# The first gating of a gated recurrence and feed-forward kernel: 384 tokens in halves of 192 instead of 512 in halves of 256

## The chip, the cores and the metric

The kernel runs on one core of one Trainium2 chip. The metric is device time in microseconds (us) of a whole execution: before the change 511.12 us, the median of three runs (511.03 to 511.22). The five engines have short names in the profile: PE is TensorE, DVE is VectorE, ACT is ScalarE, POOL is GpSimd, and SP is the engine whose queue issues nearly all the transfers here. PEld is TensorE's loading of weights.

## The reference

A gated linear recurrence runs over 4 sequences of 5824 tokens with 256 channels, and its output goes through a feed-forward network in which two projections are multiplied.

```python
log_a = 8.0 * sigmoid(r_gate) * log(clip(sigmoid(a_param)))
a_t = exp(log_a)
x_gated = sqrt(max(1 - a_t * a_t, 1e-6)) * sigmoid(i_gate) * x
h = a_t[:, t] * h + x_gated[:, t]      # for every token t; h is 0 at a sequence's start
h_ffn = (h @ w1) * (h @ w2) @ w3       # 256 -> 1024, 1024 -> 1024
out = h_ffn @ w_out                    # 1024 -> 256
```

## The kernel before, in words

All 23296 tokens stand in one row and are cut into chunks. Chunks 0 and 1 have 256 tokens each, chunks 2 to 45 have 512, and chunk 46 has 256. Chunks 0 and 1 are gated together: they share their loads, their gates and their buffers (`gates_of`, `width`), but root, gating product, scan and cast are done for each half by itself, so that the first half can go on to TensorE while the second is scanned.

Matrices w3 and w_out are multiplied with each other once, on the chip ("folding"), so that a chunk needs two stages of matmuls: up, with w1 and w2, and down, with the folded product. Channels lie on partitions and tokens run along the free axis; a gate is loaded with tokens on partitions and is turned, either by TensorE (chunks in `TURN_R` and `TURN_U`) or by a transposing transfer.

Nothing in the order is automatic. The string `ORDER` lists every job, and each engine and the transfer queue take their jobs in that order. A job's letter, its chunk and its part make a word:

- `r`, `i`, `x` load the three inputs (L151), `Lw1.1` and the like load half of w1 or w2, half of w_out, or an eighth of w3 into a staging buffer (L407). All of these are issued by SP, one after another.
- `Cw..` casts a staged weight to bf16: on ACT (L414) if in `W_ACT`, on DVE (L416) if in `W_DVE`, else on POOL.
- `R`, `I` are the two tanh, `V`, `U` the turns (L200 on TensorE), `d` the exponential (L223), `s` the square (L231, L233), `q` the root (L238), `p`, `t` build i_gate's part times x (L173, L192), `g` is the gating product (L248, L251), `h` the scan (L270), `y` the cast of the scan (L280, L282).
- `a`, `b` are the up matmuls with w1 and w2 (L299) of a quarter of the 1024 columns, `c` moves a's sums out of PSUM (L320, L322), `m` multiplies them with b's (L337), `D` is the down stage (L357), `e` and `o` move its sums out and store them.
- `Ft`, `Fc`, `Fm`, `Fe` fold one eighth of w3: transpose (L425), copy, product with w_out (L436), and scaling into `wp_sb` (L470, L472). Every `D` needs all eight.
- `W` is two matmuls on the identity (L287), whose results nobody reads.

Sets such as `DV_COPY`, `AC_SQUARE` or `DV_CAST` say which engine takes a job. `HALVED` says for how many of the four quarters the up stage of chunks 0 and 1 is run half by half; the other quarters wait for both halves and take the whole width. `RINGS` gives the number of buffers: the PSUM ring `po` has four, shared by `a`, turns, folding and `D`, and `pb` has two, shared by `b` and `W`; a job that takes a slot waits until the slot's last reader is done.

Of the kernel before, what the change touches and what calls it, by code (L numbers as in the profile page):

```python
# [23 lines left out]
def kernel(  # L24
# [25 lines left out]
    CT = 512  # L50
    sizes = [256, 256] + [512] * 44 + [256]
# [44 lines left out]
    FOLD_ACT = {('e', 0), ('e', 4), ('e', 5), ('e', 7)}
    FOLD_DMA = set()
    W_ACT = {('w2', 0), ('w3', 3)}
    W_DVE = {('w1', 1)}
# [4 lines left out]
    HALVED = 4  # L104
# [24 lines left out]
    def width(c):  # L129
        return CT if c == 0 else sizes[c]  # L130

    def part(c):
        return slice(sizes[0], CT) if c == 1 else slice(0, sizes[c])
# [37 lines left out]
    def plus(c):  # L171
        t = T["thi", c][:, :sizes[c] // P, :]
        (nc.vector if c in DV_PLUS else nc.gpsimd).tensor_scalar(t, t, 1.0, 1.0, op0=ALU.add, op1=ALU.mult)  # L173

# [115 lines left out]
    def in_half(c, mp):  # L290
        return c < 2 and mp < HALVED

# [181 lines left out]
    def last(c):  # L474
# [21 lines left out]
        r0 i0 x0 Lw1.1 Lw1.0 r2 i2 Lw2.0 Lw3.2 x2 E W13 A3. A0. A1. A2. R0.1 R0.0 W3 W10 V0.0 V0.1 I0 t0.1 d0.0 s0.0  # L496
        d0.1 s0.1 q0.0 t0.0 Cw1.1 q0.1 Cw1.0 R2 I2 W5 W8 W0 U0 W4 W11 W6 W12 W7 W9 W2 g0 h0.1 h0.0 y0.1 y0.0 a0.0.1
        a0.1.1 a0.1.0 a0.0.0 V2 W15 Cw2.0 g1 h1.1 h1.0 y1.1 y1.0 d2.1 Lw2.1 Lwo.1 Lwo.0 r3 Cw3.2 d2.0 s2.1 s2.0 q2
        b0.0 c0.0.0 c0.1.0 a1.1.0 m0.0 Ft2 a1.1.1 c1.1.0 b0.1 a1.0.0 a0.2.1 a1.0.1 b1.1 m0.1 Fc2 b1.0 a0.2.0 p2 t2.0
        t2.1 U2 c1.0.0 m1.1 Cw2.1 m1.0 a0.3.1 W14 b0.2 a1.3.1 W1 a1.3.0 c0.2.0 g2 Cwo.1 Cwo.0 r4 Lw3.0 Lw3.5 i3 Lw3.1  # L500
        Lw3.4 x3 Lw3.3 Lw3.6 Lw3.7 r7 m0.2 h2.0 h2.1 R3 a1.2.1 a1.2.0 a0.3.0 c1.3.0 c0.3.0 Fm2 b0.3 b1.2 V3 R4 V4
        c1.2.0 d3.1 d4.0 d3.0 d4.1 m0.3 b1.3 y2 Fe2 m1.2 m1.3 a2.0.0 a2.0.1 b2.0 a2.1.0 c2.0.1 c2.0.0 c2.1.0 m2.0
        Cw3.0 s3.1 Cw3.5 Cw3.1 b2.1 a2.2.1 Ft0 a2.1.1 Fc0 Ft1 c2.1.1 Fc1 s4.0 I3 s4.1 c2.2.1 a2.2.0 Ft5 Fm0 p3 Cw3.4
        c2.2.0 Fc5 m2.1 s3.0 q3 Cw3.3 Fe0 b2.3 Fm1 q4 Fe1 Ft4 t3.0 t3.1 U3 Fc4 g3 h3.0 h3.1 Cw3.6 Cw3.7 b2.2 Fm5 Fm4
        a2.3.1 Ft7 R7 Fe5 Fe4 Fc7 r5 i4 r6 x4 i5 i6 i7 c2.3.1 a2.3.0 Ft3 R5 I4 c2.3.0 Fc3 Ft6 Fm7 y3 a3.2.1 Fc6 Fm3
        m2.3 R6 Fe7 c3.2.1 V7 m2.2 Fe3 d7.1 a3.2.0 c3.2.0 d7.0 b3.2 Fm6 a3.3.1 a3.0.0 a3.3.0 m3.2 Fe6 c3.0.0 I5 c3.3.1
        s7.0 I6 V5 r8 i8 V6 r9 x5 b3.3 d5.1 a3.0.1 d5.0 c3.0.1 c3.3.0 m3.3 p4 t4.0 t4.1 p5 s7.1 U4 a3.1.1 c3.1.1 s5.0
        I7 I8 D0.1 D0.0 b3.0 b3.1 a3.1.0 g4 h4.0 h4.1 s5.1 R8 R9 d6.0 d6.1 p6 y4 p8 t5.0 t5.1 D0.3 D0.2 m3.0 e0.0
        c3.1.0 a4.1.1 b4.1 a4.3.1 D2.0 D2.1 s6.1 q7 e2.0 q5 s6.0 x6 p7 t6.0 t6.1 c4.1.1 e0.1 m3.1 c4.3.1 x7 x8 o0.0
        i10 r11 V9 o2.0 a4.0.1 a4.1.0 c4.0.1 c4.1.0 m4.1 a4.2.0 b4.3 a4.3.0 U5 g5 h5.0 h5.1 c4.2.0 c4.3.0 q6 D2.3 D2.2  # L510
        e2.1 r12 r10 V8 o2.1 o0.1 i9 i11 x10 a4.0.0 U6 D3.0 a4.2.1 D3.1 b4.0 c4.0.0 I10 c4.2.1 e3.0 d9.1 d9.0 m4.3 g6
        y5 t8.1 t7.1 t7.0 m4.0 a5.1.0 b4.2 a5.1.1 a5.0.1 a5.0.0 b5.0 c5.1.1 c5.1.0 c5.0.0 m4.2 h6.1 U7 a5.3.1 c5.0.1
        s9.1 R10 c5.3.1 R11 d8.1 I9 m5.0 g7 h6.0 b5.1 D3.3 b5.3 D3.2 a5.2.1 a5.3.0 e3.1 R12 d8.0 m5.1 c5.2.1 c5.3.0
        h7.1 D4.2 a5.2.0 D4.3 e4.1 m5.3 i13 V10 o3.0 x9 p10 t8.0 y6 p9 s8.0 s9.0 h7.0 b6.0 a6.0.0 a6.0.1 y7 c5.2.0 I11
        I13 a6.2.1 a6.2.0 b5.2 s8.1 c6.0.0 c6.0.1 c6.2.0 D4.1 a6.1.0 D4.0 d10.1 c6.2.1 d10.0 e4.0 q9 a6.1.1 m6.0 m5.2
        U8 o3.1 i12 r15 V11 r13 t9.1 t9.0 U9 V12 a6.3.0 b6.1 c6.1.1 c6.1.0 m6.1 a6.3.1 b6.2 a7.1.1 b6.3 a7.1.0 m6.2
        t10.0 s10.1 p11 t10.1 o4.0 o4.1 r16 i14 i16 c6.3.0 q8 c6.3.1 m6.3 g8 h8.0 h8.1 g9 c7.1.1 c7.1.0 a7.3.0 a7.0.0
        a7.0.1 b7.1 c7.3.0 R15 c7.0.0 c7.0.1 D6.0 D6.1 a7.3.1 D5.0 D6.2 b7.3 D6.3 D5.1 d11.1 c7.3.1 e6.0 s11.1 I12
        d11.0 d12.1 m7.1 h9.1 y8 a7.2.1 a8.2.0 b7.0 e6.1 m7.3 p12 s11.0 p13 s10.0 e5.0 a8.2.1 a7.2.0 c7.2.1 I16 c8.2.1
# [145 lines left out]
```

## Time and profile before

| | us |
|---|---|
| median of three runs | 511.12 |
| the profiled execution itself | 510.87 |
| its span (first to last instruction) | 509.1 |
| TensorE busy, of which | 501.7 |
| matmuls on the identity (`W`) | 10.7 |
| ACT busy | 461.5 |
| DVE busy | 431.8 |
| POOL busy | 318.0 |

The profiled execution took 1.8 us more than its span, and stands 0.25 us under the median. TensorE's busy time includes the `W` matmuls, so 99% busy does not mean 99% useful. A matmul's printed duration overlaps with the next one's: matmuls in a row start closer together than they last. The same holds to a smaller degree for the other engines: copies of 512 columns on DVE print 0.68 us and start 0.60 us apart. Sums of work are therefore made from the distance between starts.

### The profile page before, as it was taken

The numbers are of one execution on the slowest core, as the hardware profiler recorded it, in microseconds if no ns is written. First come the engines' busy times: TensorE is split into PE (matmuls) and PEld (weight loads), VectorE is DVE, ScalarE is ACT, GpSimd is POOL, SyncE is SP. The second block draws the span as 40 slices with busy tenths as digits, with TensorE's granted clock in tenths as the row PEclk, the third lists the DMA queues.
The fourth block names the chain that finished last, engine by engine and source line by source line (L and its number), as shares of the span: only waits on it lengthen the run. The fifth ranks groups of instructions, "written<-read, shape, count | busy, mean of one in ns | idle before, by whom it ended". The sixth has DMA issues, their size and how long they took to land.

```text
span 509.1 us, 8891 instructions
## 1 busy us (share of the span) xinstructions
PE 501.7 (99%) x3225; PEld 308.3 (61%) x3225; DVE 431.8 (85%) x417; ACT 461.5 (91%) x708; POOL 318.0 (62%) x269
## 2 busy tenths in 40 slices
PE   7999999999999999999999999999999999999997
PEld 3767665665665656556656556565566655656566
DVE  6999999999999789879979799878877797959762
ACT  7999999998999999999999999998998979888543
POOL 1686677658658937964886973956647568580200
PEclk9999999999999999999999999999999999999999
DMA  8999999999989998896999997899886895252213
GB/s 317 410 411 345 335 316 282 305 286 259 310 220 298 279 285 247 211 302 196 247 305 327 254 286 148 252 243 227 210 246 164 235 298 161 85 166 62 65 51 104
DMA packets 178048, 124.06 MB, mean 244 GB/s; under 512 B 87378, under 2 KB 174036, under 8 KB 178004
## 3 DMA queue, kind: packets, MB, share of 16 engines
q1 hardware_dynamic: 178000, 123.50, 85.4%
q8 instruction: 25, 0.41, 0.4%
q14 instruction: 19, 0.16, 0.1%
q10 hardware_dynamic: 4, 0.00, 0.0%
HBM read 78.91 MB, written 23.86 MB: 202 GB/s over the span
## 4 chain that ended last, share of the span: by engine, by line
PE 92%; ACT 3%; DMA 2%; POOL 1%; DVE 1%; issue 1%; SPq 1%; ACTq 0%; DVEq 0%
PE po L357 30%; PE pb L299 29%; PE pa L299 29%; DMA wf<-in_moe_w_dram 2%; PE pw L436 1%; ACT sa L322 1%; PE ptr L200 1%; PE ptw L425 1%; POOL u_t L192 0%; DVE h_t L270 0%; SPq L151 0%; ACT ot L322 0%; SPq L407 0%; ACT L168 0%; ACT L238 0%
## 5 line engine op out<-in xcount | busy, mean ns | idle before, releaser
L337 DVE TENSOR_TENSOR g_t<-sa,pb 128x1024 bf16<-128x1024 bf16 (+1 forms) x188 | 218.7, 1180 | 58.9 <-PE pb L299 27.6
L299 PEld LDWEIGHTS <-w_sb 128*128 128x128 bf16 x1504 | 146.4, 98 | 144.1 <-issue 1.4
L322 ACT CAST sa<-pa 128x512 bf16<-128x512 f32 (+1 forms) x332 | 179.8, 591 | 27.1 <-PE pa L299 18.9
L299 PE MATMUL pa<-y_t,w_sb 128*128 128x512 bf16 (+1 forms) x752 | 190.2, 372 | 0.2 <-ACT sa L322 0.2
L299 PE MATMUL pb<-y_t,w_sb 128*128 128x512 bf16 (+1 forms) x752 | 184.9, 372 | 0.2 <-ACT w_sb L414 0.2
L357 PE MATMUL po<-wp_sb,g_t 128*128 128x256 bf16 (+1 forms) x1464 | 177.6, 272 | 0.0
L357 PEld LDWEIGHTS <-g_t 128*128 128x128 bf16 x1464 | 142.5, 98 | 39.5 <-issue 0.3
L282 POOL CAST y_t<-h_t 128x1024 bf16<-128x1024 f32 (+2 forms) x47 | 53.8, 1145 | 140.2 <-DVE h_t L270 136.1
L192 POOL TENSOR_TENSOR u_t<-i_t,x_t 128x512 bf16<-128x512 f32 (+1 forms) x90 | 123.3, 1387 | 3.8 <-DMA ut<-u_t 1.8
L270 DVE TENSOR_TENSOR_SCAN h_t<-a_t,h_t,nrm 128x512 f32<-128x512 f32 (+1 forms) x92 | 121.1, 1343 | 1.6
L233 POOL TENSOR_TENSOR nrm<-a_t 128x512 f32<-128x512 f32 x70 | 78.4, 1137 | 7.0 <-ACT a_t L223 4.0
L223 ACT ACTIVATE a_t<-rt,la 128x512 f32<-128x512 bf16 (+1 forms) x82 | 66.1, 823 | 0.0
L322 ACT COPY ot<-po 128x512 f32<-128x512 f32 x84 | 49.1, 589 | 13.2 <-PE po L357 12.9
L173 POOL TENSOR_SCALAR i_t<-i_t 128x1024 f32<-128x1024 f32 (+1 forms) x45 | 55.4, 1233 | 8.3 <-ACT i_t L168 8.3
L251 DVE SCALAR_TENSOR_TENSOR nrm<-nrm,ut 128x1024 f32<-128x1024 f32 (+1 forms) x39 | 53.2, 1365 | 5.2 <-ACT nrm L238 5.2
L168 ACT ACTIVATE i_t<-i_t 128x1024 f32<-128x1024 f32 (+1 forms) x46 | 48.5, 1063 | 0.3 <-DMA i_t<-in_i_gate_dram 0.2
L238 ACT ACTIVATE nrm<-nrm 128x1024 f32<-128x1024 f32 (+1 forms) x47 | 48.4, 1040 | 0.2
L162 ACT ACTIVATE th_r<-r_t 128x1024 bf16<-128x1024 f32 (+1 forms) x41 | 43.5, 1064 | 0.0
L320 DVE CAST sa<-pa 128x512 bf16<-128x512 f32 x36 | 23.5, 684 | 1.4 <-PE pa L299 0.8
L238 ACT ACT_TABLE_LOAD x17 | 21.8, 1283 | 0.4
L287 PE MATMUL warm<-ident 128*128 128x512 bf16 x32 | 10.7, 473 | 1.6 <-DVE ident L441 1.6
L231 ACT ACTIVATE nrm<-a_t 128x512 f32<-128x512 f32 x18 | 11.4, 645 | 0.0
(55 smaller groups left out, 122.1 us busy)
## 6 DMA issues: line engine op xcount, KB each, us to landing
r_t<-in_r_gate_dram SPq DMA_DIRECT2D x45, 512.0 KB, 5.2
i_t<-in_i_gate_dram SPq DMA_DIRECT2D x45, 512.0 KB, 6.0
x_t<-in_x_dram SPq DMA_DIRECT2D x45, 512.0 KB, 5.5
out_dram<-ot SPq DMA_DIRECT2D x90, 256.0 KB, 3.9
wf<-in_moe_w_dram SPq DMA_DIRECT2D x12, 512.0 KB, 10.5
wf<-in_moe_w_out_dram SPq DMA_DIRECT2D x2, 512.0 KB, 10.2
rt<-th_r SPq DMA_TRANSPOSE x41, 4.7
ut<-u_t SPq DMA_TRANSPOSE x39, 4.4
```

Of the source, the lines that this page charges most:

```text
L173: (nc.vector if c in DV_PLUS else nc.gpsimd).tensor_scalar(t, t, 1.0, 1.0, op0=ALU.add, op1=ALU.mult)
L192: (nc.vector if (c, half) in DV_HALF else nc.gpsimd).tensor_mul(out=u, in0=t, in1=xt)
L223: nc.scalar.activation(out=a, in_=pr, func=AF.Exp, scale=la4[:, cb:cb + 1], bias=la4[:, cb:cb + 1])
L233: (nc.vector if (c, cb) in DV_SQUARE else nc.gpsimd).tensor_mul(out=n, in0=a, in1=a)
L238: nc.scalar.activation(out=n, in_=n, func=AF.Sqrt, scale=-1.0, bias=1.0)
L251: nc.vector.scalar_tensor_tensor(out=n, in0=n, scalar=1e-3, in1=T["pu", c][:, :, cols], op0=ALU.max, op1=ALU.mult)
L270: nc.vector.tensor_tensor_scan(h[:, cb, :], a[:, cb, :], n[:, cb, :], init, ALU.mult, ALU.add)
L282: (nc.vector if key in DV_CAST else nc.gpsimd).tensor_copy(out=y, in_=h)
L299: nc.tensor.matmul(out=dst, lhsT=w_sb[:, cb, m * P:(m + 1) * P], rhs=T["y", gates_of(c)][:, cb, span(c, mp)], start=(cb == 0), stop=(cb == ...
L322: nc.scalar.copy(out=dst, in_=src_ps)
L337: nc.vector.tensor_mul(out=T["g", z][:, 2 * mp:2 * mp + 2, span(c, mp)], in0=T["sa", c, mp][:, :, :w], in1=T["pb", c, mp][:, :, :w])
L357: nc.tensor.matmul(out=po, lhsT=T["g", c][:, k, j * P:(j + 1) * P], rhs=wp_sb[:, k, cols], start=(k == 0), stop=(k == KD - 1), skip_group_ ...
```

## The change

The sizes become 192, 192, 44 times 512, and 384. The first gating so takes 384 tokens. `HALVED` goes from 4 to 2, and `width` and `part` no longer assume that the first two chunks fill 512. The sets that assign jobs to engines, and the order, are new up to chunk 14; from there the order is the old one but for one load that moves (`r23`), and for the three pieces that the last chunk's down stage now has (`D46.2 e46.2 o46.2`).

```diff
-    sizes = [256, 256] + [512] * 44 + [256]
+    sizes = [192, 192] + [512] * 44 + [384]
...
-    DV_PLUS = set()
-    DV_HALF = set()
-    DV_SQUARE = {(0, 0), (0, 1), (5, 1), (9, 0)}
+    DV_PLUS = {2}
+    DV_HALF = {(15, 0)}
+    DV_SQUARE = {(0, 0), (0, 1)}
...
-    DV_CAST = {(1, 1)}
-    AC_CAST = {(1, 0)}
+    DV_CAST = {(1, 0), (1, 1), 2}
+    AC_CAST = set()
...
-    FOLD_ACT = {('e', 0), ('e', 4), ('e', 5), ('e', 7)}
+    FOLD_ACT = {('c', 1), ('c', 6), ('c', 7), ('e', 2), ('e', 3), ('e', 4), ('e', 5), ('e', 6), ('e', 7)}
...
-    W_ACT = {('w2', 0), ('w3', 3)}
-    W_DVE = {('w1', 1)}
+    W_ACT = {('w1', 1), ('wo', 0)}
+    W_DVE = {('w1', 0), ('w2', 0), ('w3', 1), ('w3', 6)}
...
-    HALVED = 4
+    HALVED = 2
...
     def width(c):
-        return CT if c == 0 else sizes[c]
+        return sizes[0] + sizes[1] if c == 0 else sizes[c]
...
     def part(c):
-        return slice(sizes[0], CT) if c == 1 else slice(0, sizes[c])
+        return slice(sizes[0], width(0)) if c == 1 else slice(0, sizes[c])
...
-        r0 i0 x0 Lw1.1 Lw1.0 r2 i2 Lw2.0 Lw3.2 x2 E W13 A3. A0. A1. A2. R0.1 R0.0 W3 W10 V0.0 V0.1 I0 t0.1 d0.0 s0.0
-        d0.1 s0.1 q0.0 t0.0 Cw1.1 q0.1 Cw1.0 R2 I2 W5 W8 W0 U0 W4 W11 W6 W12 W7 W9 W2 g0 h0.1 h0.0 y0.1 y0.0 a0.0.1
-        a0.1.1 a0.1.0 a0.0.0 V2 W15 Cw2.0 g1 h1.1 h1.0 y1.1 y1.0 d2.1 Lw2.1 Lwo.1 Lwo.0 r3 Cw3.2 d2.0 s2.1 s2.0 q2
...
+        r0 i0 A3. E A0. A1. A2. R0.1 R0.0 I0 x0 W8 W4 W12 V0.1 V0.0 d0.1 t0.1 t0.0 W1 U0 W9 W5 d0.0 s0.0 s0.1 q0.0 g0
+        h0.1 W7 W14 W13 W15 W6 W0 W11 h0.0 q0.1 x2 i2 r2 r3 R2 I2 Lw1.0 g1 h1.1 h1.0 y1.1 y1.0 Cw1.0 y0.1 y0.0 V2
+        a1.0.1 a1.1.0 a1.1.1 a1.0.0 a0.1.1 a0.1.0 Lw2.0 p2 Cw2.0 Lw1.1 R3 d2.0 d2.1 t2.0 s2.1 t2.1 Cw1.1 s2.0 q2 W10
+        b0.1 c1.0.0 c0.1.0 m0.1 a0.0.1 b1.0 W2 a0.3.0 c1.1.0 m1.0 c0.3.0 a0.0.0 b1.1 a0.3.1 c0.0.0 b0.0 U2 a0.2.0
+        a0.2.1 m1.1 m0.0 Lw3.2 Lwo.1 Lw2.1 Lwo.0 Cw3.2 r4 Lw3.1 Cw2.1 Cwo.1 c0.3.1 g2 c0.2.0 c0.2.1 Cwo.0 Ft2 W3 Fc2
```

Read for SP alone, the loads come in this order. Before: r0 i0 x0, w1 (second half), w1 (first half), r2 i2, w2 (first), w3.2, x2, w2 (second), w_out twice, r3 r4, w3.0 and so on. After: r0 i0 x0 (three quarters of their former size), x2 i2 r2 r3, w1 (first), w2 (first), w1 (second), w3.2, w_out.1, w2 (second), w_out.0, r4, w3.1, w3.0 and so on. `DV_COPY` grows from 36 to 40 entries, `DV_EVAC` shrinks from 7 to 6, and `AC_SQUARE` from 18 to 12. TensorE has two transposes less for each of the two turns of the first gating, 16 fewer up matmuls, and the same 182 down pieces.

## The prediction

> **What bounds the kernel now.** I read the page first: busy shares, then the chain that ended last.
>
> ```profile
> span 509.1 us, 8891 instructions
> PE 501.7 (99%) x3225; PEld 308.3 (61%) x3225; DVE 431.8 (85%) x417; ACT 461.5 (91%) x708; POOL 318.0 (62%) x269
> PE 92%; ACT 3%; DMA 2%; POOL 1%; DVE 1%; issue 1%; SPq 1%; ACTq 0%; DVEq 0%
> ```
>
> TensorE carries the chain. The table of PE by stretches says where it is not full:
>
> ```profile
> 26.40:86.00 59.60, 59.60 (x446) 1.00 1.08 346
> 326.00:386.00 60.00, 59.82 (x365) 1.00 0.84 211
> 446.00:506.00 60.00, 59.97 (x405) 1.00 0.31 87
> ```
>
> From 26.4 us on PE never rests for long. So the change can act only through the amount of matmul work, through what happens before 26.4 us, or by opening new gaps. The PE timeline of the start shows the gaps of now:
>
> ```profile
> 13.11 1.04 PE L299 MATMUL pa<-y_t,w_sb 128*128 128x256 bf16 x8
> ...
> 14.43 0.59 PE L287 MATMUL warm<-ident 128*128 128x512 bf16 x2
> 15.22 0.61 PE L299 MATMUL pb<-y_t,w_sb 128*128 128x256 bf16 x4 [0.19 <-ACT w_sb L414]
> ...
> 16.47 0.62 PE L425 MATMUL ptw<-ident,w_t 128*128 128x128 bf16 x8 [0.43 <-POOL w_t L416]
> ...
> 20.07 0.51 PE L200 MATMUL ptr<-ident,u_t 128*128 128x128 bf16 x6 [0.46 <-POOL u_t L192]
> ...
> 23.04 1.04 PE L436 MATMUL pw<-wo_sb,w3t 128*128 128x256 bf16 x8
> ...
> 26.38 1.02 PE L299 MATMUL pa<-y_t,w_sb 128*128 128x512 bf16 x4
> ```
>
> The first up matmul is at 13.11, the first of chunk 2 at 26.38. Between them are three waits and three `W` (0.43 each). Casts of weights, thus their transfers, end two of the waits.
>
> **The measure.** PE is full afterwards, so I compare what it has lost when chunk 2 begins: elapsed time less useful work. Distances between matmul starts in the trace: 0.056 us for 128 columns, 0.109 for 256, 0.216 for 512. Before, done by 26.38: 16 turns of the first gating 0.90, 64 up matmuls of 256 columns 6.98, 32 turns V2, U2, V3, V4 1.79, `Ft2` 0.45, `Fm2` 0.87: together 10.99, lost 15.39.
>
> **Work.** After, the first gating turns 12 blocks instead of 16: -0.22. Up matmuls of both odd-sized ends: before 96 x 0.109 = 10.46; after 32 of 192 columns and 48 of 384, at 0.082 and 0.163 by scaling, 10.44. Down pieces have the same columns. Work falls by 0.24.
>
> **Transfers.** SP issues all loads in one row. The trace's landings of the first fifteen, 512 KB each: 4.27, 5.58, 6.98, 9.02, 10.29, 11.55, 12.81, (about 14.07), 15.32, 16.58, 17.89, 19.23, 20.58, 21.82, 23.67. That is a saturated row, one per 1.26 us. After, the first three count 0.75 each, but x2, i2, r2, r3 now stand ahead of w1. By place in the row (w1.0 ends at 2.25 + 5 = 7.25 units, and so on): x0 6.0, r2 10.6, r3 11.9, w1.0 13.1, w2.0 14.4, w1.1 15.6, w3.2 16.9, w_out.1 18.2, w2.1 19.6, w_out.0 20.9, r4 22.3, w3.1 24.0.
>
> **Head.** r0 and i0 come 0.3 and 0.6 earlier, and DVE's and ACT's pieces are three quarters as long. Root of the first half ends at 8.7 instead of 9.9, the scan of both halves at 11.7, both casts at 12.2. But w1.0 lands at 13.1 and takes 0.69 to cast on DVE: the first up matmul is at 13.9, 0.8 later than before. The gain in the gates is spent waiting for a weight.
>
> **From there to chunk 2**, engine by engine, with these rows (durations; starts in a row are about 0.08 closer):
>
> ```profile
> L320 DVE CAST sa<-pa 128x512 bf16<-128x512 f32 x10 | 6.7, 685 | 0.9 <-PE pa L299 0.8
> L337 DVE TENSOR_TENSOR g_t<-sa,pb 128x512 bf16<-128x512 bf16 x8 | 5.2, 675 | 0.0
> L337 DVE TENSOR_TENSOR g_t<-sa,pb 128x1024 bf16<-128x1024 bf16 x5 | 6.0, 1211 | 0.0
> L270 DVE TENSOR_TENSOR_SCAN h_t<-a_t,h_t,nrm 128x512 f32<-128x512 f32 x4 | 4.9, 1276 | 0.0
> L414 ACT CAST w_sb<-wf 128x1024 bf16<-128x1024 f32 x1 | 1.0, 1045 | 0.2 <-DMA wf<-in_moe_w_dram 0.2
> ```
>
> (1) DVE from 13.1: cast w1.0, `p2` (new here), cast w2.0, then eight copies and products of 384 elements. At starts 0.60 apart for 512 and 1.13 for 1024, 384 takes 0.47. So 3 x 0.6 + 8 x 0.47, from 13.2: 18.8-19.3 with the waits between. `p2` on DVE has no row; the cast of the same size is 0.69, POOL's `p` 1.05; I take 0.69, and the other end would add 0.36, which (2) covers.
> (2) ACT: `R2` after r2 and a table load 11.7, `I2`, `R3`, two exponentials to 14.9, cast w1.1 when it lands 16.7, square, table load 1.28, root `q2` 19.5, three copies of 384 to 20.7, then the cast of w_out.0 as it lands at 20.9: 22.0.
> (3) PE does what it has by 20.4 and then waits: `Fm2` stands ahead of `b0.3`, `V3`, `b0.2` in its queue and needs w_out.0. `Fm2` at 22.05, `b0.3`, `V3`, `b0.2` to 24.7. `Ft1` needs w3.1, cast on DVE 24.0 to 24.7; then `V4`; chunk 2 begins at 25.65.
> (4) DVE meanwhile: `g2` after `q2`, `Fc2`, scan, cast w3.1, `y2` at 25.3. In time by 0.3.
>
> Done by 25.65: 12 turns 0.67, up 2.62 + 2.61, turns 1.79, `Ft2` and `Ft1` 0.90, `Fm2` 0.87: 9.46; lost 16.2. Against 15.39: +0.8; with the work -0.24: **+0.55 us**. The first gating is done sooner, but it holds 128 tokens less for PE to do (1.7 us of up work) while it waits for the rest.
>
> **Later.** I carried the queues on in the same way to 52 us. PE always finds its next job, but often with only 0.1 to 0.3 us to spare: `a2.2.1` against the exponential of chunk 4, `Fm4` and `Fm5` against their copies on DVE, `Ft6` against ACT. Moving the copies and scalings of folding to ACT and six squares off it is covered by the full PE queue; uncovered, each costs its own 0.4 to 1.0. From chunk 14 the order is the old one, so the present gaps there (0.75 us in all between 236 and 417) stay. At the end the last product, now of 768 elements, ends about 0.4 us before `D46.0` wants it (0.5 before); uncovered it costs up to 0.9. One store and its issue more lie beside the last down pieces.
>
> **A rule against the change.** The Trainium skill, "VectorE: DVE Perf Modes", section "The TRN2 errata — SBUF-src ops pay a fixed extra latency per instruction", gives an fp32 product of N elements (N+151)/0.96 ns and advises tiles of 512 or more. For 384 that is 0.56 us against the 0.47 that I drew from starts in a row. The nine pieces of 384 would take 5.0 instead of 4.2, and `y2` would end at about 25.9 and not 25.3: the end moves by +0.3, as 0.3 of it was spare. The trace's own overlap between instructions decides, but the spare is thin.
>
> **The rivals.** *DVE becomes the bound (slower).* If each DVE instruction pays its whole printed duration, then w1.0 to `y2` takes 26.05 - 13.1 and not 25.3 - 13.1, chunk 2 starts at 26.2, and in the folding the copies `Fc4`, `Fc5`, `Fc3` come late: I get gaps of 0.27, 0.15, 0.35 on PE there. Lost 16.75 + 0.8 against 15.4 + 0.1: +1.8, 512.9 us. It decides as soon as `y2` ends after 25.65. For it: DVE has no rest from 13.1 on, and in the present trace the product waits of `m` and copies run back to back. Against it: starts of 0.60 are what the trace shows.
> *The loads are a place earlier (faster).* The step from 6.98 to 9.02 is 0.8 longer than the others; if it falls away and w_out.0 and w3.1 come 1.26 earlier, chunk 2 begins at 24.6 (then bound by the scan and w3.1), lost 15.15: -0.5; if the gaps at 86 and 118 us (0.3) also go, -0.8: 510.3. Against it: the bytes ahead of them are fixed and the queue already moves about 410 GB/s.
> *The change doesn't do what it says*: with `HALVED` at 2, half of the up work waits for both halves anyway, and the end is as before. That is near my own forecast.
>
> **Numbers.** Forecast of +0.55 has 0.50, its own range 511.2 to 512.3; the DVE rival 0.33; the faster one 0.17. From the median of 511.12: 511.7; the profiled execution would be 511.4 by its own 510.87. Range 510.2 to 513.1. A difference under 0.2% (1.02 us) cannot well be told from none here; faster than 510.1 gets 0.13, between 0.52, slower than 512.14 0.35.
>
> **What would show it.** The first up matmul at 13.9 and released by the cast of w1.0 on DVE; an idle PE before `pw` until about 22, ended by ACT's cast of `wo_sb`; chunk 2 at 25.6; PE full from there. Wrong if the first up matmul is before 13, if `pw` starts before 21.5, or if PE shows gaps of over 0.5 us between 26 and 130 us.

## The result, and the profile after

The changed kernel takes 514.07 us (median of 4 runs, 513.48 to 514.31) against 511.17 (511.03 to 511.34, 4 runs) of the kernel before on the same chip: ratio 1.0050, 95% interval 1.0038 to 1.0062, 2.9 us slower. The forecast was 511.7 with a range of 510.2 to 513.1. The profiled execution of the changed kernel took 514.31 us, 3.44 more than that of before.

First the page of the changed kernel: span, busy time of the engines, shares of the chain that ended last.

```profile
span 512.5 us, 8844 instructions
PE 502.5 (98%) x3205; PEld 306.7 (60%) x3205; DVE 431.5 (84%) x417; ACT 461.0 (90%) x704; POOL 317.6 (62%) x271
PE 84%; DVE 6%; ACT 4%; issue 3%; POOL 1%; DMA 1%; SPq 0%; DVEq 0%; ACTq 0%; POOLq 0%
```

PE carried 92% of the chain before and carries 84% now; DVE has gone from 1 to 6%. The waits for DVE are not all at the start, as PE by stretches shows (stretch, its length, PE busy, matmuls, granted clock, share of the DMA engines, GB/s):

```profile
26.80:86.00 59.20, 59.20 (x436) 1.00 1.07 324
86.00:146.00 60.00, 58.95 (x367) 1.00 1.04 283
146.00:206.00 60.00, 59.90 (x368) 1.00 0.98 272
```

The first stretch is full, as forecast. The second lacks 1.05 us, where the kernel before lacks nothing:

```profile
86.00:146.00 60.00, 60.00 (x373) 1.00 1.04 276
```

Now the PE timeline of the start:

```profile
9.08 5.74 PE L287 MATMUL warm<-ident 128*128 128x512 bf16 x18
15.10 1.15 PE L299 MATMUL pa<-y_t,w_sb 128*128 128x192 bf16 x12
...
21.29 0.61 PE L425 MATMUL ptw<-ident,w_t 128*128 128x128 bf16 x8 [0.42 <-ACT sa L322]
21.73 0.59 PE L287 MATMUL warm<-ident 128*128 128x512 bf16 x2
22.99 1.03 PE L436 MATMUL pw<-wo_sb,w3t 128*128 128x256 bf16 x8 [0.67 <-ACT wo_sb L414]
...
26.82 1.03 PE L299 MATMUL pa<-y_t,w_sb 128*128 128x512 bf16 x4
```

The first up matmul is at 15.10 (13.11 before) and the first of chunk 2 at 26.82 (26.38 before), with 1.5 us less work done by then. The wait ahead of `pw`, ended by ACT's cast of `wo_sb`, is the announced one, 0.9 us late.

The measure is the prediction's: elapsed time less useful matmul work. (A few per cent of the matmul records are missing in the traces; a hole of exactly one matmul's length is counted as that matmul.) "y2" is the end of the last vector job that chunk 2's up matmuls need, "work" the useful work done when they begin.

| kernel | us | ratio (95%) | y2 ends | chunk 2 | work | lost there | lost at 46 | at 146 | at 500 us |
|---|---|---|---|---|---|---|---|---|---|
| before | 511.1 | | 26.33 | 26.38 | 11.0 | 15.3 | 15.5 | 15.7 | 16.1 |
| after | 514.07 | 1.0050 (1.0038-1.0062) | 26.46 | 26.82 | 9.5 | 17.3 | 17.3 | 19.0 | 20.0 |
| e1, after again | 513.53 | 1.0042 (1.0030-1.0054) | 25.92 | 26.27 | 9.5 | 16.8 | 16.9 | 18.6 | 19.0 |
| e2, new order, 256 | 513.83 | 1.0052 (1.0040-1.0065) | 27.64 | 28.14 | 11.5 | 16.7 | 16.9 | 18.6 | 19.0 |
| e3, old order, 192 | 513.49 | 1.0043 (1.0029-1.0058) | 26.35 | 26.70 | 9.1 | 17.6 | 17.7 | 19.6 | 20.3 |
| e4, m11.3 first | 512.61 | 1.0025 (1.0018-1.0033) | 25.75 | 26.11 | 9.5 | 16.6 | 16.6 | 17.3 | 18.4 |
| e12, y12 on ACT | 512.85 | 1.0030 (1.0019-1.0040) | 26.28 | 26.64 | 9.5 | 17.1 | 17.2 | 18.3 | 18.8 |
| e5, Fm2 late | 512.60 | 1.0027 (1.0017-1.0038) | 26.44 | 26.80 | 9.5 | 17.3 | 17.3 | 17.9 | 19.0 |
| e6, and w3.1 on POOL | 513.27 | 1.0044 (1.0032-1.0056) | 25.62 | 27.48 | 9.5 | 18.0 | 18.2 | 18.6 | 19.2 |
| e7, r3 late | 512.86 | 1.0038 (1.0027-1.0050) | 26.16 | 26.52 | 9.7 | 16.8 | 16.8 | 17.5 | 18.5 |
| e9, Ft1 late | 513.83 | 1.0050 (1.0037-1.0062) | 25.44 | 25.61 | 9.1 | 16.5 | 18.4 | 19.0 | 19.7 |
| e10, Ft1, Fm2 late | 514.53 | 1.0064 (1.0051-1.0077) | 25.43 | 25.67 | 9.1 | 16.6 | 19.5 | 20.3 | 21.2 |
| e11, scan sooner | 513.22 | 1.0039 (1.0027-1.0051) | 25.52 | 25.57 | 8.6 | 16.9 | 17.3 | 17.9 | 18.6 |
| e15, the same on ACT | 514.45 | 1.0058 (1.0044-1.0071) | 25.08 | 25.13 | 8.8 | 16.3 | 18.2 | 18.6 | 19.3 |
| e13, three gates | 513.33 | 1.0039 (1.0026-1.0053) | 25.16 | 25.21 | 8.6 | 16.6 | 18.2 | 18.8 | 19.3 |
| e14, the same, 256 | 514.57 | 1.0064 (1.0052-1.0077) | 27.32 | 27.39 | 10.6 | 16.8 | 18.5 | 19.2 | 19.8 |

Ratios are to runs of before on the same chip. The sum closes. In the profiled execution of after, lost time at 500 us is 3.83 above before (19.97 - 16.14), work 0.24 below, and the stretch from the last matmul to the end 0.15 shorter: 3.44, as measured. Of the 3.83, 1.96 are there when chunk 2 begins and 1.87 come later. In the repeat it is 1.42 and 1.44, less 0.39: 2.47 us, and its profiled execution is 2.46 above before's.

### The profile page after: what moved, and what is told of

Same layout as the page of the kernel before. It is cut to its first block, busy times and chain, and to the rows that moved or that the text cites. A ratio compares the mean times of both kernels' runs of the same rounds, so it can differ in the third digit from the quotient of the medians.

```text
span 512.5 us, 8844 instructions
## 1 busy us (share of the span) xinstructions
PE 502.5 (98%) x3205; PEld 306.7 (60%) x3205; DVE 431.5 (84%) x417; ACT 461.0 (90%) x704; POOL 317.6 (62%) x271
## 4 chain that ended last, share of the span: by engine, by line
PE 84%; DVE 6%; ACT 4%; issue 3%; POOL 1%; DMA 1%; SPq 0%; DVEq 0%; ACTq 0%; POOLq 0%
PE po L357 28%; PE pb L299 26%; PE pa L299 26%; DVE g_t L337 3%; DVE h_t L270 2%; ACT sa L322 2%; PE warm L287 1%; PE pw L436 1%; DMA x_t<-in_x_dram 1%; POOL u_t L192 1%; PE ptr L200 1%; PE ptw L425 1%; DVE sa L320 1%; ACT ot L322 1%; ACT i_t L168 1%
## 5 line engine op out<-in xcount | busy, mean ns | idle before, releaser
L337 DVE TENSOR_TENSOR g_t<-sa,pb 128x1024 bf16<-128x1024 bf16 (+2 forms) x186 | 218.3, 1190 | 60.4 <-PE pb L299 30.5
L322 ACT CAST sa<-pa 128x512 bf16<-128x512 f32 (+1 forms) x328 | 178.4, 593 | 31.7 <-PE pa L299 22.5
L299 PE MATMUL pa<-y_t,w_sb 128*128 128x512 bf16 (+2 forms) x744 | 188.6, 374 | 0.2 <-ACT sa L322 0.2
L299 PE MATMUL pb<-y_t,w_sb 128*128 128x512 bf16 (+2 forms) x744 | 184.3, 374 | 0.8 <-DVE g_t L337 0.8
L192 POOL TENSOR_TENSOR u_t<-i_t,x_t 128x512 bf16<-128x512 f32 x89 | 123.2, 1400 | 9.4 <-DVE i_t L173 3.2
L270 DVE TENSOR_TENSOR_SCAN h_t<-a_t,h_t,nrm 128x512 f32<-128x512 f32 (+2 forms) x90 | 117.8, 1338 | 1.5
L233 POOL TENSOR_TENSOR nrm<-a_t 128x512 f32<-128x512 f32 x78 | 87.6, 1139 | 12.4 <-ACT a_t L223 11.7
L322 ACT COPY ot<-po 128x512 f32<-128x512 f32 (+1 forms) x86 | 49.9, 586 | 11.5 <-PE po L357 11.1
L173 POOL TENSOR_SCALAR i_t<-i_t 128x1024 f32<-128x1024 f32 (+1 forms) x44 | 51.7, 1181 | 7.1 <-ACT i_t L168 7.1
L238 ACT ACTIVATE nrm<-nrm 128x1024 f32<-128x1024 f32 (+2 forms) x47 | 48.4, 1041 | 2.4 <-DVE nrm L233 1.5
L320 DVE CAST sa<-pa 128x512 bf16<-128x512 f32 (+1 forms) x40 | 25.7, 666 | 1.1 <-PE pa L299 0.4
```

Of the source, the lines that this page charges most:

```text
L192: (nc.vector if (c, half) in DV_HALF else nc.gpsimd).tensor_mul(out=u, in0=t, in1=xt)
L233: (nc.vector if (c, cb) in DV_SQUARE else nc.gpsimd).tensor_mul(out=n, in0=a, in1=a)
L238: nc.scalar.activation(out=n, in_=n, func=AF.Sqrt, scale=-1.0, bias=1.0)
L270: nc.vector.tensor_tensor_scan(h[:, cb, :], a[:, cb, :], n[:, cb, :], init, ALU.mult, ALU.add)
L299: nc.tensor.matmul(out=dst, lhsT=w_sb[:, cb, m * P:(m + 1) * P], rhs=T["y", gates_of(c)][:, cb, span(c, mp)], start=(cb == 0), stop=(cb == ...
L322: nc.scalar.copy(out=dst, in_=src_ps)
```

## The experiments

**1. Size and order apart.** e1 is the changed kernel again; e2 takes its order and engines with the old sizes; e3 the old order and engines with the new sizes. `HALVED` goes with the order: it is 2 in e2 and 4 in e3.

```diff
 e2, on the changed kernel
-    sizes = [192, 192] + [512] * 44 + [384]
+    sizes = [256, 256] + [512] * 44 + [256]
-        ... D0.2 ...
+        ... D0.2 D0.3 ...
-        ... D46.0 D46.1 D46.2 e46.0 e46.1 e46.2 o46.0 o46.1 o46.2
+        ... D46.0 D46.1 e46.0 e46.1 o46.0 o46.1
 e3, on the kernel before: the reverse
```

> The changed kernel once more, for a second trace. In the first one x of the first gating landed at 7.55 us, 2.7 us after i, with single packets of up to 1.6 us, and one scan of 2.15 us (else 1.28) stood before a TensorE gap of 0.98 us at 138.7 us. If both belong to the kernel, they come again and the time is 513.5 to 514.3. If they are chance, x lands near 6.0, TensorE begins chunk 2 about 1 us earlier than at 26.8, and the gap at 138.7 is gone from the trace.

> The new order and assignment, but with the old sizes (256, 256, 512..., 256; D0.3 put beside D0.2). Size theory (the smaller first gating leaves TensorE 1.7 us less work while it waits for the same loads): the loss shrinks by what the larger gating gives back, 1.7 us less the 0.95 us that its larger loads take: 513.3. Order theory (weights stand behind four inputs of later chunks in the row of loads, and the jobs up to chunk 14 are worse placed): no better than the changed kernel, 514 or more, since nothing of the order is undone.

> The old order and assignment, but with the new sizes (192, 192, 512..., 384; D0.3 left out, D46.2 added, all four quarters in halves). Every load after the first three is 0.95 us earlier, TensorE has 1.7 us less to do before chunk 2 and 0.25 us less in all. Order theory: within 0.7 us of the kernel before, 511.0 to 511.9, so that nearly all of the loss is the order's. Size theory: most of the loss stays, 513 or more.

e1 repeats the result, 0.5 us lower, with x0 landing at 7.13 instead of 7.55; the gap of 0.98 us near 139 us, which experiment 2 is about, comes again. e2 and e3 each cost as much as the whole change: size and order do not add up. e2's time lies between what its two theories said, and e3's is what the size theory said. In e3, y2 ends when it does before, although the first gating is a quarter smaller. The POOL timelines of before and of e3 show this cast:

```profile
25.28 1.04 POOL L282 CAST y_t<-h_t 128x1024 bf16<-128x1024 f32 x1 [2.32 <-DVE h_t L270]
```

```profile
25.31 1.04 POOL L282 CAST y_t<-h_t 128x1024 bf16<-128x1024 f32 x1 [2.31 <-DVE h_t L270]
```

So under the old order the smaller first gating takes 1.9 us of work away from TensorE and moves the next chunk by nothing: +2.3 us lost. And e3 loses 1.9 us more between 46 and 146 us, where the kernel before loses 0.2, though the jobs there are in the old order; its longest gaps, 0.56 at 54 us and 0.53 at 140 us, are ended by POOL's cast of a scan's result. So a loss behind the start does not belong to the new order alone. In the new order the sizes make no difference to lost time (16.8 and 16.7 at chunk 2, 18.6 and 18.6 at 146 us). The smaller size needs another order to be worth anything, and this order, at equal sizes, begins chunk 2 with 1.3 us more lost than the old one. In e2 the loads of chunk 2 come up to 8 us sooner than before, but DVE, between the first gating and chunk 2's gate, has two casts of weights and `p2` to do besides copies and products, about 1.8 us. The gate starts at 22.20, and y2 ends at 27.64. In the kernel before, where no such job stands between, the gate starts at 20.94.

**2. The gap at 139 us.** e4 swaps two neighbours in DVE's row.

```diff
-        ... h12.1 y12 h13.0 m11.3 h13.1 ...
+        ... h12.1 y12 m11.3 h13.0 h13.1 ...
```

> The changed kernel with one word moved: the product m11.3 ahead of the scan h13.0 in DVE's queue. In the trace m11.3 waited behind that scan, which POOL's cast of y12 slowed from 1.28 to 2.15 us, and TensorE stood 0.98 us at 138.7 us for its PSUM slot. If TensorE bounds there: 0.9 us faster than the changed kernel, 513.1. If DVE and ACT bound that stretch themselves, the gap comes back a few us later and the time stays at 514.0.

e12 leaves that order and takes the POOL cast away that runs beside the scan:

```diff
-    AC_CAST = set()
+    AC_CAST = {12}
```

> The changed kernel with one cast, y12, moved from POOL to ACT. In the changed kernel the scan h13.0 runs while POOL makes this cast and takes 2.15 us instead of 1.28; behind it m11.3 is late and TensorE waits 0.98 at 138.7. In e4_product_first the product m11.3 runs beside the same cast and takes its usual 1.20. Theory P (a scan on DVE stops while POOL casts): the scan takes 1.28 to 1.35, the gap at 138.7 shrinks to under 0.2, and the time falls by up to 0.8, less what ACT's extra 1.06 us costs (0 to 0.4): 513.0. Rival (the scan is slow at this place for another reason, or the order alone makes m11.3 late): the scan takes 2.1 again or the gap stays over 0.5, and the time is within 0.3 of the repeat, 513.5, or above.

In the changed kernel the PE timeline has one long wait at 138.7 us and a shorter one 9 us earlier, and DVE and POOL show what is ahead of the long one:

```profile
129.92 1.91 PE L357 MATMUL po<-wp_sb,g_t 128*128 128x256 bf16 x16 [0.23 <-DVE sa L320]
...
138.73 1.02 PE L299 MATMUL pb<-y_t,w_sb 128*128 128x512 bf16 x4 [0.82 <-DVE g_t L337]
```

```profile
134.04 3.53 DVE L270 TENSOR_TENSOR_SCAN h_t<-a_t,h_t,nrm 128x512 f32<-128x512 f32 x2
137.49 1.19 DVE L337 TENSOR_TENSOR g_t<-sa,pb 128x1024 bf16<-128x1024 bf16 x1
```

```profile
135.45 1.04 POOL L282 CAST y_t<-h_t 128x1024 bf16<-128x1024 f32 x1 [4.57 <-DVE h_t L270]
```

(Measured between starts, TensorE loses 0.40 and 0.98 at these two places; the idle time in brackets is 0.16 shorter, because a matmul's printed end lies that far behind the moment at which the next could start.) The two scans `h12.1` and `h13.0` take 3.53 us together, 1.28 and 2.15 with 0.1 between them; the cast `y12` begins with the second and keeps its 1.04. `m11.3` starts 0.87 late and TensorE waits for it. DVE of e4 (product, then two scans) and of e12 (two scans, then the product):

```profile
134.52 1.20 DVE L337 TENSOR_TENSOR g_t<-sa,pb 128x1024 bf16<-128x1024 bf16 x1
135.63 2.45 DVE L270 TENSOR_TENSOR_SCAN h_t<-a_t,h_t,nrm 128x512 f32<-128x512 f32 x2
```

```profile
133.84 2.67 DVE L270 TENSOR_TENSOR_SCAN h_t<-a_t,h_t,nrm 128x512 f32<-128x512 f32 x2
136.42 1.19 DVE L337 TENSOR_TENSOR g_t<-sa,pb 128x1024 bf16<-128x1024 bf16 x1
```

In e4 the product runs beside the same POOL cast and keeps 1.20; the scans take 2.45 for both. In e12 they take 2.67 with the cast on ACT. The gap of 0.98 is gone in e4 and 0.12 in e12, which pays 0.35 back in small waits just after. Most of the gain lasts to the end: e4 is 0.9 us under the repeat, e12 0.7. That shows the cause of about 0.9 of the 2.9 us: a scan that POOL's cast holds up, with a product behind it that TensorE waits for. The Trainium skill states it, "SBUF — State Buffer", section "SBUF: two separate sides": DVE and GpSimd share a pair of ports under an exclusive lock; a DVE operation with two inputs in SBUF and a GpSimd operation that reads SBUF exclude each other, and whichever starts later waits for the whole of the other. The scan has two inputs in SBUF; the product takes one of its two from PSUM. Scan and product in the trace behave as that says, with 0.87 of a cast of 1.04. The wait at 129.9 is in every kernel with the new order that was profiled, with 0.4 to 0.7 us (e8, with another order there, has other gaps); taking it away was not tried, and its cause stays open.

**3. The later gaps all at once (inconclusive).** e8 takes the changed order up to the first up matmul of chunk 4 and then the remaining jobs in the old order, on the engines of the kernel before (the sets are left out here).

```diff
-        ... m3.3 a4.1.1 R9 c4.3.0 b3.0 a4.3.1 ...
+        ... m3.3 b3.0 R9 d6.0 d6.1 D0.2 m3.0 a4.1.1 ...
```

> The changed kernel's order and engines up to the first up matmul of chunk 4 (about 50 us), from there the remaining jobs in the order of the kernel before, on its engines. Theory O (the later gaps, 0.4 at 130, 1.0 at 139 and 0.4 at 193 us, belong to the new order of chunks 4 to 14): TensorE's lost time grows by about 0.3 us between 46 and 300 us, as it does before, instead of 2.2, and the time is about 1.7 us below the changed kernel's, 511.9. Rival S (any order that is late at the start, or that was laid out for other sizes, meets such gaps): the growth is 1.5 us or more in other places, and the time 513.3 or more. The old order with 192-token halves grew by 2.0, which speaks for S.

It took 529.02 us (ratio 1.0347, 1.0334 to 1.0361). At 68.6 us TensorE waits 9.9 us for a DVE copy that waits for an output tile to be stored; in the spliced row of transfers that store stands behind loads and turning transfers that the other half wanted first. What it was to test, it cannot tell.

**4. The start: one gate at a time.** All on e4. e5 puts the product `Fm2` behind other ready work, e6 also moves the cast of w3.1 off DVE, e7 loads r3 behind the weights, e9 takes w3.1 out of the way of chunk 2, e10 also `Fm2`.

```diff
 e5 and e6
-        ... Fc2 Fm2 b0.3 V3 b0.2 R4 ...
+        ... Fc2 b0.3 V3 b0.2 Fm2 R4 ...
 e6 also
-    W_DVE = {('w1', 0), ('w2', 0), ('w3', 1), ('w3', 6)}
+    W_DVE = {('w1', 0), ('w2', 0), ('w3', 6)}
 e7
-        ... x2 i2 r2 r3 R2 ... Lw1.1 R3 d2.0 ... Lwo.0 Cw3.2 r4 ... b0.3 V3 b0.2 R4 ...
+        ... x2 i2 r2 R2 ... Lw1.1 d2.0 ... Lwo.0 Cw3.2 r3 r4 ... b0.3 b0.2 R3 V3 R4 ...
 e9
-        ... i3 Cw3.1 Ft1 V4 Fc1 y2 a2.1.1 a2.3.1 m0.3 ...
+        ... i3 y2 Cw3.1 V4 a2.1.1 a2.3.1 Ft1 Fc1 m0.3 ...
 e10: e9 and the edit of e5
```

> From here on the kernels are made on e4_product_first (512.61 us, ratio 1.0025). The product Fm2, which waits 0.83 us for the cast of w_out.0, goes behind b0.3, V3 and b0.2 in TensorE's queue. My theory: three gates end at nearly the same time at the start of chunk 2 (the cast of w_out.0 on ACT 22.2, the cast of w3.1 on DVE 25.1, y2 on DVE 25.75), so the gap of 0.83 ahead of pw moves to the one ahead of Ft1, and chunk 2 starts where it did, 26.1 (+-0.15): time within 0.2 us of e4. Rival, as my prediction read it (Fm2 is the place where time is lost): chunk 2 starts 0.5 to 0.8 us sooner and the time falls by as much, to 512.0.

> As e5_fold_product_late, and the cast of w3.1 goes from DVE, where it stands behind the two scans of chunk 2, to POOL, which is idle from 21.6 to 26.3 in e4. This clears the second gate and moves the third: y2 ends at 25.1 instead of 25.75, Ft1 can run from 24.5. My theory (three gates at once): chunk 2 starts at 25.4 to 25.6, 0.5 to 0.7 before e4, and TensorE's lost time falls by as much by 27 us; the time is 512.0 if nothing later takes it back. Rival (ACT is the engine that paces chunk 2: Fc1 behind d3.1, then Fm1): the start moves, but a gap of 0.4 or more opens ahead of Fm1 or of a2.2, and the time stays within 0.2 us of e4's.

> As e4_product_first, but the load r3, which the new order of transfers puts ahead of all weights, goes behind the last piece of w_out, and R3 and V3 follow it to just ahead of R4 and behind b0.2. Each weight piece then lands one place (1.26 us) sooner: w1.1 at 14.35, w2.1 at 18.3, w_out.0 at 19.6. Theory L (the order of transfers makes the loss at the start): the gap of 0.61 ahead of a0.0.1 and that of 0.83 ahead of pw shrink to under 0.3 each, chunk 2 starts at 25.1 to 25.4, 0.7 to 1.0 us before e4, and the time is about 511.8. Rival A (ACT's row of gates sets the end, in whatever order it is loaded): R3 only moves along ACT's row, d3 and Fc1 come as late as before or 0.5 later, and chunk 2 or the folding after it (Fm1) loses again what the start gained: time within 0.3 us of e4.

> On e4_product_first (512.61 us, 1.0025). The earlier traces put the end of the start on w3.1: it is the sixteenth transfer and lands at 24.4 to 25.2, Ft1 waits for its cast and stands ahead of V4 and of chunk 2 in TensorE's queue. Here y2 goes ahead of the cast of w3.1 on DVE, and Ft1 and Fc1 behind a2.3.1. Theory G (w3.1 is the last gate): the gap ahead of ptw goes, chunk 2 starts at y2's end, 25.1 to 25.4 instead of 26.1, lost time at 27 us is 16.2 to 16.4 instead of 16.6 (Ft1's 0.45 of work is then still to do), and Fm1 waits 0.2 more for Fc1: 512.3. Rival (the row of gates on ACT and DVE is the bound in any arrangement): chunk 2 starts at 25.1 all the same, but what was gained is lost at Fm1 or a2.2: lost time at 46 us as in e4, 16.6, and 512.6.

> As e9_transpose_late, and Fm2 behind b0.2 as in e5_fold_product_late, so that neither w_out.0 nor w3.1 stands ahead of other ready work. Theory G: TensorE has no gap of over 0.3 at pw; the only gap left is the one ahead of chunk 2, which then starts with y2 at 25.1; lost time at 27 us 16.1, another 0.1 to 0.2 under e9, 512.2. Rival: as e9, nothing more.

e5: the wait at `pw` is gone, one of 1.84 stands ahead of `Ft1` instead, and the time is e4's. e6 did not do what my theory said: y2 came at 25.62, but with the cast on POOL, which sat idle for 3.1 us before it, `Ft1` still came at 26.58. The cast had to wait for the load of w3.1, at 25.2. e7 did bring ACT's root `q2` a microsecond sooner (19.08 instead of 20.15), and DVE then shows the same wait:

```profile
21.07 2.45 DVE L270 TENSOR_TENSOR_SCAN h_t<-a_t,h_t,nrm 128x512 f32<-128x512 f32 x2
24.87 0.69 DVE L416 CAST w_t<-wf 128x1024 bf16<-128x1024 f32 x1 [1.35 <-DMA wf<-in_moe_w_dram]
25.48 0.69 DVE L282 CAST y_t<-h_t 128x1024 bf16<-128x1024 f32 x1
```

The scans of chunk 2 are done at 23.5, and y2 stands behind a cast that waits for w3.1; the time stays within 0.3 us of e4's. e9 removes that: chunk 2 starts at 25.61 and `Ft1` does not wait. But what was gained is lost at once. The PE timeline of e9:

```profile
29.59 1.03 PE L436 MATMUL pw<-wo_sb,w3t 128*128 128x256 bf16 x8 [1.58 <-ACT a_t L223]
```

`Fm1` needs one of the four PSUM slots of its ring. The ring goes by order of use, so with `Ft1` behind `V4` it is now `V4`'s slot, free only when ACT has made the second exponential from it. e10 has the same wait and two more. Neither theory of e9 and e10 had the slot in it, and both kernels are over a microsecond slower than e4.

**5. The start: several gates together.** e11 is e10 with `V4` behind `Ft1`, the cast of w_out.0 on POOL and the copy `Fc2` on ACT; e15 is e11 with the cast of w_out.0 back on ACT. e13 is e7 with `y2` and `m0.3` ahead of the cast of w3.1, and `Ft1`, `Fc1`, `V4` and `a2.2.1` between `b2.1` and `Fm1`; e14 is e13 with the sizes of before.

```diff
 e11, on e10 (e15: the FOLD_ACT line and the order only)
-    W_ACT = {('w1', 1), ('wo', 0)}
+    W_ACT = {('w1', 1)}
-    FOLD_ACT = {('c', 1), ('c', 6), ...
+    FOLD_ACT = {('c', 1), ('c', 2), ('c', 6), ...
-        ... y2 Cw3.1 V4 a2.1.1 a2.3.1 Ft1 Fc1 ...
+        ... y2 Cw3.1 a2.1.1 a2.3.1 Ft1 V4 Fc1 ...
 e13, on e7 (e14: with the old sizes)
-        ... R3 V3 R4 d3.0 Fe2 d3.1 h2.1 h2.0 ... i3 Cw3.1 Ft1 V4 Fc1 y2 a2.1.1 a2.3.1 m0.3 c2.1.1 c2.3.1 m0.2 b2.1 Fm1 d4.0 d4.1 I3 a2.2.1 ...
+        ... R3 Fe2 V3 R4 d3.0 d3.1 h2.1 h2.0 ... i3 y2 m0.3 Cw3.1 a2.1.1 a2.3.1 c2.1.1 c2.3.1 m0.2 b2.1 Ft1 Fc1 V4 a2.2.1 Fm1 d4.0 d4.1 I3 ...
```

> As e10_transpose_and_product_late, and the row that leads to y2 is cleared too: the cast of w_out.0 goes from ACT to POOL, the copy Fc2 from DVE (where it stands ahead of chunk 2's scans) to ACT, and V4 behind Ft1. Theory G plus its last member (y2 on DVE behind 0.69 us of Fc2): y2 ends at 24.4 to 24.7, chunk 2 starts there, lost time at 27 us 15.8 to 16.1, within 0.5 of the kernel before, and the time is 511.9 to 512.1. Rival (fewer tokens to work on cannot be made up for by any arrangement): y2 moves, but TensorE then waits for Ft1, V4 or Fm1, lost time at 46 us stays at 16.5 or more and the time at 512.5 or more.

> On e7_gate3_late (r3, R3 and V3 behind the weights; q2 ends at 19.1 there and the scans of chunk 2 at 23.5): y2 and m0.3 go ahead of the cast of w3.1 on DVE, and Ft1, Fc1 and V4 behind b2.1 on TensorE, with a2.2.1 ahead of Fm1, so that Fm1's PSUM slot is not V4's; Fe2 goes ahead of R4. Theory O (several gates in series, all made by the new order): y2 ends at 24.2, chunk 2 starts at 24.3 to 24.6, TensorE has no gap of over 0.5 from there to 46 us, lost time at 46 us is 15.9 to 16.2 (16.6 in e4, 15.5 before), the time 511.9 to 512.1. Rival T (too few tokens to fill the wait, in any order): lost time at 46 us stays at 16.6 or more, the wait appearing ahead of Ft1, V4 or Fm1, and the time at 512.6 or more.

> As e13_three_gates with the sizes of before (256, 256, 44 x 512, 256). Theory O: the size itself is worth little; the first gating ends 0.5 to 0.8 later, TensorE has 1.7 us more of up work meanwhile, and lost time at 46 us is within 0.3 of e13's; the time is e13's +-0.4, with the 0.24 of additional matmul work in it. Rival T: the 128 tokens fill the wait, lost time at 46 us is at least 0.5 under e13's and the time 0.3 or more under it.

> As e11_scan_sooner, but the cast of w_out.0 stays on ACT, so that no POOL cast runs beside the scans of chunk 2; Fc2 follows it on ACT. The scans take 1.26 each, y2 ends at 24.7 to 25.0 (25.52 in e11) and chunk 2 starts there. Theory D (DVE's row to y2 is the bound of the start): nothing takes it back, lost time at 46 us is 16.5 or less (17.3 in e11, 16.6 in e4, 15.5 before), 512.3 us. Theory B (DVE and ACT are both full, work moved from one to the other comes out there): ACT is a microsecond later with R4, d3 and Fc1, TensorE waits 0.5 or more at Fm1, a2.2 or the next foldings, lost time at 46 us is 17 or more and the time 513 or more.

In e11 y2 ended at 25.52, not 24.4 to 24.7. DVE's scans and POOL's casts of that time:

```profile
21.52 3.27 DVE L270 TENSOR_TENSOR_SCAN h_t<-a_t,h_t,nrm 128x512 f32<-128x512 f32 x2
```

```profile
20.77 2.95 POOL L416 CAST wo_sb<-wf 128x1024 bf16<-128x1024 f32 x2
```

Two scans usually take 2.45 and two such casts 2.03 (start of one to end of the other). Here they take turns: the second cast, 1.96 long, gets through when the first scan is over, and the second scan, 1.99 long, when that cast is. The lock again, 0.8 us of it on the path. In e15 the earlier POOL cast (w_out.1) still ran beside the first scan, which took 1.70; y2 ended at 25.08, and TensorE then waited 1.37 at `Ft1` for a slot that a DVE copy frees. In e13 y2 ended at 25.16, and 0.39 at `Fm1` and 0.99 at 31.4 took it back. e14 has the same lost time at chunk 2 and at 46 us within 0.3 us, so the 128 tokens are not what is missing in this order either. It is 1.2 us slower than e13, more than was expected; 0.24 of that is work, and the rest was not followed up.

Across e4 to e15, e14 with its larger sizes apart, y2 moves between 25.1 and 26.5, and lost time at chunk 2 hardly does (16.3 to 17.3, 18.0 in e6). In e9 to e15 the table shows why: what was moved out of the way, `Ft1` above all, is then missing from the work done (8.6 to 9.1 instead of 9.5 us). By 46 us none of them is below e4's 16.6. Removing gates brought nothing back; that an order exists for these sizes that does is not excluded. No kernel here beats the one before; e4 and e5 come nearest.

## Why the prediction was wrong, step by step

Two steps failed. At the start the row of jobs that leads to y2 and to chunk 2 was mis-sized: ACT and the loads were late, and 0.8 us of loss became 1.96 (1.42 in the repeat). And the stretch from 52 us to chunk 14, which the forecast put at nothing without following it, held most of the other half of the loss. The sign was right in part by luck: that fewer tokens leave TensorE with less to do is what e3 shows under the old order, but e2 has the same loss with the old sizes.

- **Work, -0.24:** right, 489.66 to 489.42 us. The tail was right too: the stretch from the last matmul to the end is 3.2 us, 3.35 before.
- **Transfers ("the first three count 0.75 each"):** the first step that failed. x0 landed at 7.55 instead of 6.0 (6.2 to 7.5 in the traces with 192-token halves), and everything behind it some 0.6 late: r2 11.23 for 10.6, w2.0 15.04 for 14.4, w_out.0 21.58 for 20.9. Three quarters of the bytes took as long as the whole; in e3 the fourth load lands at 8.98, before at 9.02. For w3.1 I had 24.0; it came at 25.14. In e4, whose start is the same program, x0 landed at 6.34 and the row was nearly as forecast (r2 10.47, w_out.0 20.86), but w3.1 came at 24.43 and chunk 2 at 26.11, still 0.46 late: the rest of the miss is not x0's.
- **The first up matmul, 13.9 by w1.0's cast:** at 15.10, behind `W` jobs and `V2`. TensorE had stood 2.3 us idle for x0, its `W` matmuls then ran 0.43 apart, at half rate, up to 13 us. In e4 it is 13.82. Up to there the miss is x0.
- **(1) DVE:** the sizes were right. Pieces of 384 start 0.47 apart (17.56, 18.02), `p2` takes 0.69. The sum counts eight of them where nine run ahead of the gate; they are done by 20.6 all the same, before `q2`. The rule that I weighed is stated on its page for an fp32 add; its estimate of 0.56 for 384 agrees with the duration of these copies and products (0.56 and 0.55 here) and not with their pace. So the slower rival's premise, that each instruction pays its whole duration, is wrong, and that its end (y2 at 26.05, chunk 2 at 26.2) was nearer than mine is chance.
- **(2) ACT, "`R2` after r2 and a table load 11.7 ... exponentials to 14.9 ... root `q2` 19.5":** too early: `q2` ends at 19.6 to 20.9 in every trace with the new order but e7's. ACT of the changed kernel:

```profile
10.86 0.52 ACT L238 ACTIVATE nrm<-nrm 128x384 f32<-128x384 f32 x1 [0.68 <-DVE nrm L248]
11.40 1.28 ACT L160 ACT_TABLE_LOAD   x1
12.69 1.06 ACT L160 ACTIVATE th_r<-r_t 128x1024 bf16<-128x1024 f32 x1
...
16.87 1.04 ACT L414 CAST w_sb<-wf 128x1024 bf16<-128x1024 f32 x1
...
19.81 1.06 ACT L238 ACTIVATE nrm<-nrm 128x1024 f32<-128x1024 f32 x1
```

I had overlooked that the second root, `q0.1`, stands behind `g0`, which writes the same tile on DVE (0.68 of waiting), and that the table load stands behind `q0.1`. `R2` begins at 12.69 instead of 10.65, and from there ACT has no rest: `q2` ends at 20.87 instead of 19.5. In e4, with the early x0, it is 20.15, still 0.65 late.
- **(4) y2 "at 25.3, in time by 0.3":** 26.46, 25.92 in the repeat. From `q2` on the working holds: DVE needs 5.6 us for gate, `Fc2`, scans, cast of w3.1 and y2, and I had 5.8. But ACT's lateness alone does not explain y2: the cast of w3.1 begins at 25.16, when the scans have just ended (25.15) and w3.1 has just landed (25.14); in e4 both are at 24.43. Each of the two alone would have held y2 there. In the two other traces with the same start, scans and landing are at 24.73 and 24.53 (repeat) and at 24.33 and 24.96 (e12), and in e7, whose `q2` is a microsecond sooner, y2 waits for w3.1. So both terms were too small, and which of them decides changes from one execution to the next.

```profile
20.90 1.29 DVE L248 SCALAR_TENSOR_TENSOR nrm<-nrm,ptr 128x512 f32<-128x512 f32 x2 [0.28 <-PE pa L299]
22.10 0.68 DVE L320 COPY w3t<-ptw 128x1024 bf16<-128x1024 bf16 x1
22.70 2.45 DVE L270 TENSOR_TENSOR_SCAN h_t<-a_t,h_t,nrm 128x512 f32<-128x512 f32 x2
25.16 0.69 DVE L416 CAST w_t<-wf 128x1024 bf16<-128x1024 f32 x1
25.77 0.69 DVE L282 CAST y_t<-h_t 128x1024 bf16<-128x1024 f32 x1
```

- **(3) `Fm2` 22.05, `Ft1` 24.75, chunk 2 at 25.65, lost 16.2:** 22.99, 25.92, 26.82 and 17.3. The wait at `pw` is where it was announced, the work done by then is 9.52 (9.46 forecast), so the 1.1 are all lateness; in the repeat, with 16.8, it is half of that. e5 shows that the wait at `pw`, which I took for the one that costs, is covered by the next.
- **"PE always finds its next job", "the present gaps stay" (to 52 us, and from chunk 14 on):** the queues were followed to 52 us, and the stretch from there to chunk 14 was taken as empty. It holds 0.40 at 129.9 and 0.98 at 138.7, the second made by a scan that POOL's cast holds up (e4, e12). DVE is busy for 30.6 of the 31 us from 109 to 140 (30.5 before), so a row without slack was there to be seen, and so was the lock. The scans of the kernel before (min, median, max in ns):

```profile
L270 DVE TENSOR_TENSOR_SCAN h_t<-a_t,h_t,nrm x92: 727/1279/2379, 13.2 to 487.8; 128x512 f32<-128x512 f32 x88, 128x256 f32<-128x256 f32 x4
```

- **"Wrong if gaps of over 0.5 between 26 and 130":** there is none in that stretch; the one of 0.98 is 9 us behind it.
- **The range:** its upper end, 513.1, came from the DVE rival. Neither it nor my own forecast had a case for a loss between 52 us and chunk 14, though the change reorders the jobs there.

## What to carry to other kernels

A smaller first tile only pays if the second tile's inputs come sooner with it: take the time of the last job that the second tile needs, subtract the work that is ready until then, and compare that; e3 lost 2.3 us with everything else unchanged. A reordered stretch has to be followed to its end, or given a price: look for the stretches where a second engine has no slack, and there for instructions that another engine can stop. Such instructions show when median and maximum of one kind are compared. When a row is rearranged by hand, follow the PSUM ring too: a slot is waited for by order of use, and moving one transpose made another job wait 1.6 us.

## What the runs showed of the hardware that was not expected

- **A scan and a POOL cast exclude each other, nearly in full.** 1.28 became 2.15 beside a cast of 1.04; in e11 both sides paid, 1.99 for the scan and 1.96 for the cast. In the changed kernel 13 of the 90 scans after 22 us take over 1.4 us (15 of 90 before), and all of them overlap a POOL instruction. About as many overlap one and stay short, and one rule covers both. If POOL's instruction is under way when a scan of 512 begins, or begins by the records at most 0.05 us after it, the scan ends 1.08 us after POOL's end. If POOL's instruction begins later, the scan keeps its 1.28, and POOL's cast or square, 1.04 us alone, ends 0.83 us after the scan. The second of the two so ends as if it had begun 0.20 us before the first one's end. Of over 500 such meetings of more than 0.25 us in sixteen traces (all but e8's), all but one keep to this within 0.02 us; in that one the two began 0.05 us apart. `h13.0` and `y12` are such a meeting: the cast begins 0.03 us behind the scan that it holds up, and ends at 136.49, the scan at 137.57.
- **The first transfers are not a row of constant speed.** Transfers by stretches of the changed kernel, of e3 and of e2 (length, granted clock, share of the DMA engines, GB/s):

```profile
5.00:6.50 1.50, 1.00 0.95 198
8.00:12.00 4.00, 0.71 1.01 406
```

```profile
5.00:6.50 1.50, 1.00 0.63 149
```

```profile
5.00:6.50 1.50, 1.00 1.01 412
```

With 192-token halves (packets of 3 KB) the rate falls to 150 to 300 GB/s from 5 to 6.5 us, single packets taking up to 1.6 us; with 256 (4 KB) in e2 it does not, nor in e14, while the kernel before, whose weights come in packets of 2 KB, has a dip at 6.5 to 8 us (298 GB/s). What makes the dip, and whether the packet size does, was not tested. The granted clock of 0.71 in the changed kernel follows TensorE's 2.3 us of waiting for x0; but the repeat, after 1.8 us of it, kept 1.00, and e10, after 2.1, had 0.64 in the same stretch. What decides was not tested.
- **A fetch of instructions sits in the row of loads.** Between 22.5 and 23.5 us the transfers of the changed kernel contain one packet of another queue:

```profile
q8 instruction: 1, 0.02, 5.9%
```

It is of 16 KB and takes 0.95 us on one of the 16 DMA engines. The loads behind it are landing 1.26 apart, but the step across it is about 2.3 (r4 at 22.88, w3.1 at 25.14), since a load has landed when its slowest engine has: fifteen of w3.1's sixteen shares were in by 24.13. The traces of before and e4 show such a packet at the same place, 1 to 2 us earlier.
